# A waiting no-operation on the sync engine behind the last store of a scaled residual add

## The chip, the core and the metric

The kernel runs on one core of a Trainium2 chip. The metric is the device time of one execution in microseconds (us). A time is the median of several runs. Beside it stands one execution under the hardware profiler, which gives the views quoted here.

## The reference

```python
B, S, D = 512, 32, 640        # x, fx: (512, 32, 640) bfloat16; alpha: (1,) bfloat16

def reference(x, fx, alpha):
    return x + alpha * fx
```

One multiply and one add for each element. `x` and `fx` are read once and the output is written once: 20.97 MB each, 62.92 MB in all.

## The kernel before

The 512 x 32 rows are laid over the chip's 128 partitions, so that each partition holds 81920 consecutive elements of `x`, of `fx` and of the output. These are cut into five units of 16384 elements (`UNIT`), 32 KB a partition and 4 MB in all for each unit.

There are two pools of large tiles with two buffers each: `wide`, whose tiles hold two units of `x`, and `fs`, whose tiles hold one unit of `fx`. `x` comes in three loads, of units 0 and 1, of units 2 and 3, and of unit 4. `fx` comes in five loads, one for each unit. The vector engine computes `fx * alpha + x` in one instruction for each unit (line 59) and writes the result over the `x` tile. The result leaves in three stores, cut like the loads of `x`: `store(0, 2)`, `store(2, 2)` and `store(4, 1)` (line 71). The value of alpha is loaded alone (line 76), spread over the 128 partitions by a matmul with a row of ones (line 80), and copied for the vector engine (line 82).

All DMAs, loads and stores alike, are issued by the sync engine (SP) through one queue. The order of the instructions on each engine is written out by hand: the body stands under `tc.manual_schedule()`, and the loop over the units is unrolled in the source (lines 73 to 99). What the kernel doesn't write are the waits. The framework puts them in from the use of the tiles: an instruction waits on semaphores, which landed DMAs and finished instructions count up. A DMA adds 16 to its semaphore, one for each of the 16 DMA engines. An instruction that needs more waits than it can carry gets further waiting instructions ahead of it, which the trace shows as `EVENT_SEMAPHORE`.

Behind the body the framework adds a closing part of its own, for which no line of the kernel's body stands. Its records carry line 124, where the framework's context is opened and left. On the sync engine it waits for everything that the program has in flight or has counted, the last store among it; then come a barrier over all five engines, the clearing of the semaphores by GpSimd (POOL), and a second barrier. Records of the opening part carry line 113.

The lines that the change touches: `load_x` (49) and `load_f` (55) issue the loads, `compute` (59) the multiply-add, `store` (71) the stores; the unrolled order follows from line 73 on and ends with `store(4, 1)`.

Of the kernel before, what the change touches and what calls it, by code (L numbers as in the profile page):

```python
# [1 line left out]

# [4 lines left out]

ACT = mybir.ActivationFunctionType
ALU = mybir.AluOpType
F32 = mybir.dt.float32  # L10
BF16 = mybir.dt.bfloat16

UNIT = 16384
P = 128


@with_exitstack
def kernel(
    ctx: ExitStack,
    tc: tile.TileContext,  # L20
    x: bass.AP,
    fx: bass.AP,
    alpha: bass.AP,
    out: bass.AP,
):

    nc = tc.nc  # L30
    xv = x.flatten_outer_dims().rearrange("(p n) d -> p (n d)", p=P)
    fxv = fx.flatten_outer_dims().rearrange("(p n) d -> p (n d)", p=P)
    ov = out.flatten_outer_dims().rearrange("(p n) d -> p (n d)", p=P)
    assert xv.shape[1] == 5 * UNIT

    consts = ctx.enter_context(tc.tile_pool(name="consts", bufs=1))
    psum = ctx.enter_context(tc.tile_pool(name="psum", bufs=1, space=bass.MemoryType.PSUM))
    wide = ctx.enter_context(tc.tile_pool(name="wide", bufs=2))
    fs = ctx.enter_context(tc.tile_pool(name="fs", bufs=2))
    ctx.enter_context(tc.manual_schedule())  # L40

    xt, ft = {}, {}

    def cols(u, n):
        return slice(u * UNIT, (u + n) * UNIT)

    def load_x(u, n):
        t = wide.tile([P, 2 * UNIT], x.dtype, tag="x", name="x_t")
        nc.sync.dma_start(out=t[:, : n * UNIT], in_=xv[:, cols(u, n)])  # L49
        for i in range(n):  # L50
            xt[u + i] = (t, i)

    def load_f(u):
        ft[u] = fs.tile([P, UNIT], fx.dtype, tag="f", name="f_t")
        nc.sync.dma_start(out=ft[u][:], in_=fxv[:, cols(u, 1)])  # L55

    def compute(u):
        t, i = xt[u]
        nc.vector.scalar_tensor_tensor(  # L59
            out=t[:, i * UNIT : (i + 1) * UNIT],  # L60
            in0=ft[u][:],
            scalar=a_f[:],
            in1=t[:, i * UNIT : (i + 1) * UNIT],
            op0=ALU.mult,
            op1=ALU.add,
        )

    def store(u, n):
        t, i = xt[u]
        assert i == 0  # L70
        nc.sync.dma_start(out=ov[:, cols(u, n)], in_=t[:, : n * UNIT])

    load_x(0, 2)

    a_1 = consts.tile([1, 1], alpha.dtype, name="a_1")
    nc.sync.dma_start(out=a_1[:], in_=alpha[None, :])  # L76
    ones = consts.tile([1, P], alpha.dtype, name="ones")
    nc.vector.memset(ones[:], 1.0)  # L78
    a_ps = psum.tile([P, 1], F32, name="a_ps")
    nc.tensor.matmul(a_ps[:], ones[:], a_1[:], start=True, stop=True)  # L80
    a_f = consts.tile([P, 1], F32, name="a_f")
    nc.vector.tensor_copy(out=a_f[:], in_=a_ps[:])  # L82

    load_f(0)
    load_f(1)
    load_x(2, 2)
    compute(0)
    load_f(2)
    compute(1)
    store(0, 2)  # L90
    load_f(3)
    load_x(4, 1)
    compute(2)
    load_f(4)
    compute(3)
    store(2, 2)
    compute(4)
    store(4, 1)


# [1 line left out]
_INS = ['x', 'fx', 'alpha']  # L102
_OUTS = [((512, 32, 640), 'bfloat16')]


# [23 lines left out]
```

## Time and profile before

| | us |
|---|---|
| time, median of 3 runs (lowest to highest) | 152.76 (152.31 to 152.86) |
| the profiled execution's own time | 152.47 |
| its span, from the first to the last instruction of the program | 150.7 |
| vector engine busy in it | 86.7 |
| issue of the last store | 138.08 |
| its landing, when the last of 16 DMA engines has counted it | 149.63 |
| landing of the store before it, `store(2, 2)` | 139.95 |

The span leaves out 1.8 us of the execution's own time, which lie before the program's first instruction and after its last. In the views an engine's name with a small q (SPq) means its sequencer, which waits, issues DMAs and handles barriers and doesn't count as busy. A group's line gives the source line, the engine, the operation, the count, and durations; a view of one source line gives durations in ns as min/median/max and the first and last start in us, rounded to tenths. The profile's chain of waits is followed back from the last instruction that an engine itself executes, and so begins before the closing part. For a DMA, "to landing" is the time from its issue by the queue to its last count.

The order in which the sync queue issues its DMAs, with their start in us: `x` units 0 and 1 (0.73), alpha (1.17), `fx` 0 and 1 (1.55, 1.94), `x` units 2 and 3 (2.82), `fx` 2 (50.08), `store(0, 2)` (67.28), `fx` 3 (67.68), `x` unit 4 (91.48), `fx` 4 (91.92), `store(2, 2)` (118.48), `store(4, 1)` (138.08).

### The profile page before, as it was taken

Reading aid. Unit: us, or ns where it says so; the run is one execution under the profiler, and the core shown is the slowest. Engines: PE = TensorE matmul, PEld = TensorE weight load, DVE = VectorE, ACT = ScalarE, POOL = GpSimd, SP = SyncE. Lnnn points to the kernel's source line nnn. Section 1 sums busy time; section 2 is a strip of 40 time slices with the busy share of each in tenths; the row PEclk is TensorE's granted clock in tenths of the full one; section 3 lists DMA queues with packets and bytes.
Section 4 is the critical chain, followed back from the end, with each engine's and each line's share of the span. In section 5 each row is a group of like instructions: output and inputs, shape, how many; then the busy total and the mean of one; then the engine's idle time right before and its main releaser. Section 6 shows DMA issues by size and latency. Waiting matters only on the chain.

```text
span 150.7 us, 75 instructions
## 1 busy us (share of the span) xinstructions
PE 0.2 (0%) x1; PEld 0.1 (0%) x1; DVE 86.7 (58%) x7; POOL 0.2 (0%) x4
## 2 busy tenths in 40 slices
PE   0000000000000000000000000000000000000000
PEld 0000000000000000000000000000000000000000
DVE  0000000039999999980899970019999499996000
POOL 0000000000000000000000000000000000000000
DMA  8899899999999896999899989999999999989993
GB/s 278 383 452 470 365 418 417 426 426 444 478 452 487 348 557 278 426 452 478 348 522 417 417 365 418 435 418 426 444 435 470 487 435 400 470 365 391 435 426 139
DMA packets 1586, 62.92 MB, mean 418 GB/s; under 512 B 178, under 2 KB 178, under 8 KB 178
## 3 DMA queue, kind: packets, MB, share of 16 engines
q1 hardware_dynamic: 1586, 62.92, 97.5%
HBM read 41.94 MB, written 20.97 MB: 417 GB/s over the span
## 4 chain that ended last, share of the span: by engine, by line
DMA 56%; DVE 34%; SPq 1%; issue 0%; DVEq 0%
DMA f_t<-in_fx_dram 40%; DVE x_t L59 34%; DMA out_dram<-x_t 16%; SPq L49 0%; SPq L76 0%; DVEq L59 0%; SPq L55 0%
## 5 line engine op out<-in xcount | busy, mean ns | idle before, releaser
L59 DVE SCALAR_TENSOR_TENSOR x_t<-f_t,a_f,x_t 128x16384 bf16<-128x16384 bf16 x5 | 86.3, 17284 | 29.0 <-DMA f_t<-in_fx_dram 29.0
L82 DVE COPY a_f<-a_ps 128x1 f32<-128x1 f32 x1 | 0.2, 157 | 21.6 <-PE a_ps L80 21.6
L78 DVE MEMSET ones<- 1x128 bf16 x1 | 0.2, 165 | 0.8 <-PEq L113 0.8
L80 PE MATMUL a_ps<-a,ones 1*128 1x1 bf16 x1 | 0.2, 158 | 22.4 <-DMA a<-in_alpha_dram 22.4
L113 POOL MEMSET const-uint8-127<- 128x1 uint8 x1 | 0.1, 102 | 0.0
L113 POOL MEMSET const-bfloat16-1.0<- 128x1 bf16 x1 | 0.1, 101 | 0.0
L80 PEld LDWEIGHTS <-ones 1*128 1x128 bf16 x1 | 0.1, 98 | 1.0 <-DVE ones L78 1.0
L113 POOL MEMSET const-float32-0.0<- 128x1 f32 x1 | 0.1, 98 | 0.2 <-issue 0.2
L113 POOL MEMSET const-float32-1.0<- 128x1 f32 x1 | 0.1, 98 | 0.0
## 6 DMA issues: line engine op xcount, KB each, us to landing
f_t<-in_fx_dram SPq DMA_DIRECT2D x5, 4096.0 KB, 32.3
x_t<-in_x_dram SPq DMA_DIRECT2D x1, 4096.0 KB, 19.4
out_dram<-x_t SPq DMA_DIRECT2D x1, 4096.0 KB, 11.6
x_t<-in_x_dram SPq DMA_DIRECT2D x2, 40.5
out_dram<-x_t SPq DMA_DIRECT2D x2, 22.8
a<-in_alpha_dram SPq DMA_DIRECT2D x1, 0.0 KB
```

The lines of the kernel that those rows point to most:

```text
L59: nc.vector.scalar_tensor_tensor(out=t[:, i * UNIT : (i + 1) * UNIT], in0=ft[u][:], scalar=a_f[:], in1=t[:, i * UNIT : (i + 1) * UNIT], op ...
L78: nc.vector.memset(ones[:], 1.0)
L80: nc.tensor.matmul(a_ps[:], ones[:], a_1[:], start=True, stop=True)
L82: nc.vector.tensor_copy(out=a_f[:], in_=a_ps[:])
L113: nc = _bacc.Bacc("TRN2", target_bir_lowering=False, num_devices=1)
```

## The change

Every load, the matmul, the first two stores and the last multiply-add are kept in a list, `done`. Behind the last store the sync engine gets a no-operation that is made to depend on each of them: on all that the program does but the last store itself. (The copies and multiply-adds that aren't listed come earlier on the vector engine than the one that is.) `compute` and `store` now return the instruction that they make. Nothing that is loaded, computed or stored is changed.

```diff
+    done = []
...
     def load_x(u, n):
         t = wide.tile([P, 2 * UNIT], x.dtype, tag="x", name="x_t")
-        nc.sync.dma_start(out=t[:, : n * UNIT], in_=xv[:, cols(u, n)])
+        done.append(nc.sync.dma_start(out=t[:, : n * UNIT], in_=xv[:, cols(u, n)]))
...
     def load_f(u):
         ft[u] = fs.tile([P, UNIT], fx.dtype, tag="f", name="f_t")
-        nc.sync.dma_start(out=ft[u][:], in_=fxv[:, cols(u, 1)])
+        done.append(nc.sync.dma_start(out=ft[u][:], in_=fxv[:, cols(u, 1)]))
...
-    nc.sync.dma_start(out=a_1[:], in_=alpha[None, :])
+    done.append(nc.sync.dma_start(out=a_1[:], in_=alpha[None, :]))
...
-    nc.tensor.matmul(a_ps[:], ones[:], a_1[:], start=True, stop=True)
+    done.append(nc.tensor.matmul(a_ps[:], ones[:], a_1[:], start=True, stop=True))
...
-    store(0, 2)
+    done.append(store(0, 2))
...
-    store(2, 2)
-    compute(4)
+    done.append(store(2, 2))
+    done.append(compute(4))
     store(4, 1)
+
+
+    rest = nc.sync.nop(nofuse=True)
+    info = mybir.DependencyInfo(mybir.DependencyClass.Sync, mybir.DependencyReason.DATA)
+    for i in done:
+        tc.add_manual_dep(rest.ins, i.ins.name, info, reason="all but the last store")
```

More of the change, by code (lines that the diff above doesn't have):

```diff
@@ L54, in load_f @@
         ft[u] = fs.tile([P, UNIT], fx.dtype, tag="f", name="f_t")
-        nc.sync.dma_start(out=ft[u][:], in_=fxv[:, cols(u, 1)])
+        done.append(nc.sync.dma_start(out=ft[u][:], in_=fxv[:, cols(u, 1)]))
     def compute(u):
         t, i = xt[u]
-        nc.vector.scalar_tensor_tensor(
+        return nc.vector.scalar_tensor_tensor(
             out=t[:, i * UNIT : (i + 1) * UNIT],
@@ L70, in store @@
         assert i == 0
-        nc.sync.dma_start(out=ov[:, cols(u, n)], in_=t[:, : n * UNIT])
+        return nc.sync.dma_start(out=ov[:, cols(u, n)], in_=t[:, : n * UNIT])
     load_x(0, 2)
     a_1 = consts.tile([1, 1], alpha.dtype, name="a_1")
-    nc.sync.dma_start(out=a_1[:], in_=alpha[None, :])
+    done.append(nc.sync.dma_start(out=a_1[:], in_=alpha[None, :]))
     ones = consts.tile([1, P], alpha.dtype, name="ones")
```

## The prediction

> **What bounds the kernel now.** I read the page's DMA part first, then the costliest groups, then the waits of the sync engine's queue, then the end of the span in small windows. From the page:
>
> ```profile
> ## 3 DMA queue, kind: packets, MB, share of 16 engines
> q1 hardware_dynamic: 1586, 62.92, 97.5%
> ...
> L59 DVE SCALAR_TENSOR_TENSOR x_t<-f_t,a_f,x_t 128x16384 bf16<-128x16384 bf16 x5 | 86.3, 17284 | 29.0 <-DMA f_t<-in_fx_dram 29.0
> ```
>
> Transfers fill 97.5% of the 16 DMA engines' span; the vector engine works 86.3 us of 150.7 and waits 29.0 us for tiles of `fx`. So DMA sets the time, up to the last landing. The chain of waits on the page ends with the last vector instruction (138.06 us) and says nothing of what follows, so I asked for the last 12.6 us separately. First the record of the last store (the view of line 71, from 130 us on), then the closing stretch by windows (columns: stretch, length, each engine's busy time, clock, DMA share, GB/s):
>
> ```profile
> L71 SPq DMA_DIRECT2D out_dram<-x_t x1: 344/344/344, 138.1 to 138.1; - x1
> ...
> DMA to landing us min/median/max: 11.6/11.6/11.6
> ```
>
> ```profile
> 138.40:149.60 11.20, 0.00 (x0) 0.00 (x0) 0.00 (x0) 0.00 (x0) 1.00 0.87 375
> 149.60:150.70 1.10, 0.00 (x0) 0.00 (x0) 0.00 (x0) 0.00 (x0) 1.00 0.00 0
> ```
>
> The store is issued at 138.08 and lands at 149.63. For 11.2 us the sync engine has nothing to do. Then follows 1.1 us in which no engine works and no byte moves: only the program's closing on line 124. The waits of the sync engine's queue say what opens it:
>
> ```profile
> SPq L124 <- DMA out_dram<-x_t: 11.2, 1, 11.2
> SPq L124 <- PEq L124: 0.6, 2, 0.4
> ```
>
> and line 124 in two short windows (149.60 to 149.95, 149.95 to 149.99) what it consists of (duration in ns min/median/max, first and last start):
>
> ```profile
> L124 SPq EVENT_SEMAPHORE  x1: 17/17/17, 149.7 to 149.7; - x1
> L124 SPq EVENT_SEMAPHORE  x4: 28/28/28, 149.7 to 149.9; - x4
> L124 SPq DRAIN  x1: 7/7/7, 150.0 to 150.0; - x1
> ```
>
> One wait for the last store, four instructions with two waits each, and a drain that carries a tenth wait. The unrounded starts in the trace's records are 149.650, 149.709, 149.770, 149.835, 149.896 and 149.961; the next instruction, the drain that reports the queue to the closing barrier, starts at 150.020. All nine other semaphores had long been complete (the latest is the store of units 2 and 3, landed 139.95), yet each instruction takes its step of (149.961 - 149.650) / 5 = 0.062 us, because they stand in the queue behind the wait for the last store.
>
> **The change part by part.** *The list `done`, the added `return`s:* Python only. No instruction for the chip, so 0.
>
> *The no-operation on the sync engine.* It brings new waits, for at most nine semaphores, those of everything but the last store: the loads of `x`, `fx` and alpha, the matmul, both earlier stores, the last multiply-add. Its own record is in no row. The nearest are the drains and waits above: 7 to 28 ns long, a step of 0.062 us. At two waits an instruction nine of them take four waiting instructions and the no-operation itself, five steps or 0.31 us, at most six or 0.37. It is issued after the last store's issue (138.08 + 0.34 = 138.42), waits until 139.95 for the earlier store, and is done by 140.3 at the latest. The cover is the last store's flight, until 149.63; 9.3 us of it are left over. Behind it in the sync engine's queue stands only the closing on line 124, which waits for the landing anyway. No DMA, no tile and no other engine waits for it. On the path: 0. Without that cover it would cost its 0.31 to 0.37 us.
>
> *What it lets go of.* If the closing then waits for the last store alone, that wait fits on the drain, which can start at about 149.65 where the first wait now starts. Five steps go: 149.961 - 149.650 = 0.311 us. The barrier, the clearing of semaphores and the second barrier (150.020 to the end, 0.67 us) shift forward unchanged: the other four engines' drains are long reached. Bounds: nothing goes if the closing repeats its waits (0); if one wait more is left, say for the no-operation's own count, four steps go (0.25); more than the five steps cannot go, as the rest answers to other engines. Taken: 0.31.
>
> Sum, against the profiled execution: 152.47 us in all, 150.7 of it span; 152.47 - 0.31 = 152.16, span 150.4. That execution was 0.29 below the median of the runs (152.76, from 152.31 to 152.86). The middle of all four executions is (152.47 + 152.76) / 2 = 152.6, less 0.31 is 152.3; the median less 0.31 is 152.45. I go between: **152.4 us**.
>
> A rule that speaks against any gain is in the Trainium skill, Perfetto Trace Analysis, section Identifying Performance Opportunities: improving a kernel generally means improving its most-contended engine. By that rule alone, with DMA untouched, the forecast would be no gain, 152.6 to 152.76. The last window's row, DMA share 0.00 for 1.1 us, shows a place where that engine is not what is waited for, and there I follow the row.
>
> **The rivals.** *The closing repeats its waits.* What the program does with a wait already made must be read off the queues. For repetition: four of the closing's waits repeat, to the same value, what this very queue had waited for before. The records name the semaphores: 106 and 101 by the wait of line 55 at 91.86 us, 107 by the load at 91.49, 105 by the wait of line 71 at 92.34, 99 by the last store; the closing asks again for 105, 106 and 107 unchanged, and for 99 at the last store's value. So what DMA issues of this queue have seen is not credited to the closing drain. Against: within the body, waits are not repeated. The `fx` load at 67.68 needs the second multiply-add finished and carries no wait for it, since the store before it did; the vector engine waits once for the first `x` tile and uses it twice. The simplest reading is that DMA issues and the engine's own instructions keep separate accounts, and a no-operation belongs, with the drain, to the second. I hold that likelier, at two to one. If it is wrong, the no-operation is hidden and nothing goes: 152.6 to 152.76, say 152.7.
>
> *The no-operation gets ahead of the last store.* Slower: one wait in the wrong place. The store would then be issued only once the earlier store has landed, at 139.95 plus a step or two instead of 138.08. Its 11.55 us of flight shift whole, for with the engines free its first data packets started 0.84 us after the issue (138.92 in the packets' records). Landing at about 151.55, so +1.92, less 0.31 of the closing: 152.6 + 1.6 = 154.2. It decides from the point at which the no-operation starts before 138.08. For it: `done` holds nothing that keeps it behind the last store. Against: every DMA of the sync queue starts in the order in which the source has it, and the no-operation is written last.
>
> *More than the five steps.* Faster by over 0.5% (0.76 us) would need 0.45 us of the 0.67 us of barrier too. The page shows no mechanism; only the scatter of the runs (0.55 us from end to end) can make it look so.
>
> **How the numbers follow.** Closing shortened by four or five steps: 0.63. Closing repeats its waits: 0.29. No-operation ahead of the store: 0.03. More than the five steps, or something else: 0.05. A measurement of this kernel can tell about 0.5% (0.76 us) from no change; both likely cases lie within it (0.2% and 0). So: within 0.5%, 0.87. Faster by more, 0.09: most of it the first case with the scatter's help, as a run at the low end, 152.31 - 0.31 = 152.0, is just at the bound. Slower by more, 0.04: the order rival and a rest.
>
> The range: at the low end the lowest run less six steps, 152.31 - 0.37 = 151.9; at the high end the highest run with no saving, 152.86, rounded up to 152.9. It holds the first two cases with their scatter and leaves the other two out.
>
> **What would show it.** Right: on line 124 of the sync queue the two-wait instructions are gone after 149.6 us and stand between 138.4 and 140.3 instead, on the no-operation's line; from the last landing to the span's end about 0.75 us instead of 1.06; the last store still issued at 138.1 with 11.6 us to landing; everything before that as it was. The second case: the same four instructions with two waits still start after the last landing, beside a no-operation near 140. The order rival: the last store issued near 140.0. The forecast is wrong if the step of 0.062 us is not what a satisfied wait costs but comes from the landing itself, or if a no-operation's waits disturb the transfers in flight: then the last store's 11.6 us would change.

## The result and the profile after

| | before | after |
|---|---|---|
| time, median of 18 runs (us) | 152.47 (152.11 to 152.87) | 152.17 (151.82 to 152.48) |
| ratio, 95% interval | | 0.9977 [0.9969, 0.9985] |
| span of the profiled execution (us) | 150.69 | 150.47 |
| issue of the last store, its landing (us) | 138.08, 149.63 | 138.11, 149.72 |
| closing: last landing to the end of the span (us) | 1.060 | 0.749 |

By the ratio the kernel became 0.35 us faster (0.23 to 0.47 by its interval), by the difference of the two medians 0.30. That is 0.2%: within the 0.5% named as the bound of no change, though the interval leaves no change out. The closing is 0.311 us shorter. The spans differ by 0.22 us only, because this execution's last landing came 0.09 us later.

What bounds the kernel is as it was. From the page of the changed kernel (its lines are numbered higher; the multiply-add is now line 60, the stores line 72, the no-operation line 102, the closing line 131; in the experiments the closing's number moves again):

```profile
q1 hardware_dynamic: 1586, 62.92, 97.7%
...
L60 DVE SCALAR_TENSOR_TENSOR x_t<-f_t,a_f,x_t 128x16384 bf16<-128x16384 bf16 x5 | 86.3, 17284 | 29.0 <-DMA f_t<-in_fx_dram 29.0
```

Same bytes, same busy time, same 29.0 us of waiting for `fx`. The last store, from the view of its line:

```profile
L72 SPq DMA_DIRECT2D out_dram<-x_t x1: 344/344/344, 138.1 to 138.1; - x1
...
DMA to landing us min/median/max: 11.6/11.6/11.6
```

It starts 0.03 us later and flies 0.06 us longer; two executions of the changed kernel itself (the first experiment) differ by 0.42 and 0.08. The windows behind it (columns as in the prediction):

```profile
138.45:149.72 11.27, 0.00 (x0) 0.00 (x0) 0.00 (x0) 0.00 (x0) 1.00 0.87 372
149.72:150.50 0.78, 0.00 (x0) 0.00 (x0) 0.00 (x0) 0.00 (x0) 1.00 0.00 0
```

The stretch without any transfer was 1.1 us long and is now 0.78. Where the waiting went, by the sync queue's waits:

```profile
SPq L131 <- DMA out_dram<-x_t: 9.5, 1, 9.5
SPq L102 <- DMA out_dram<-x_t: 1.5, 1, 1.5
SPq L131 <- PEq L131: 0.6, 2, 0.4
```

Before, line 124 waited 11.2 us in one piece. Now the no-operation's line waits 1.5 us for the earlier store and the closing 9.5 us for the last one. (A `DRAIN` is one more instruction of the engine's queue; in the closing's records one carries a wait, and the next counts up the barrier's semaphore.) The views of lines 102 and 131 (the second from 149.60 to 149.79) show the instructions (ns min/median/max, first and last start):

```profile
L102 SPq EVENT_SEMAPHORE  x5: 28/28/1493, 138.5 to 140.2; - x5
```

```profile
L131 SPq DRAIN  x1: 7/7/7, 149.7 to 149.7; - x1
```

Five waiting instructions with two waits each stand under the store's flight, and the one of 1493 ns holds the real wait. Behind the landing (149.722) one drain is left, at 149.739; the drain that reports to the barrier follows at 149.797, 0.058 us later. Before, from the first wait to that drain were six steps, 0.370 us. The rest of the closing takes 0.674 us in both. The no-operation has no record of its own: both traces hold 75 instructions, and what differs is the place of five waiting instructions and the carrier of the wait for the last store, which has gone from the first waiting instruction to the drain.

### The profile page after: what moved, and what is told of

The parts are those of the page before. It is cut to its first block, busy times and chain, and to the rows that moved or that the text cites. A ratio compares the mean times of both kernels' runs of the same rounds, so it can differ in the third digit from the quotient of the medians.

```text
span 150.5 us, 75 instructions
## 1 busy us (share of the span) xinstructions
PE 0.2 (0%) x1; PEld 0.1 (0%) x1; DVE 86.7 (58%) x7; POOL 0.2 (0%) x4
## 4 chain that ended last, share of the span: by engine, by line
DMA 56%; DVE 34%; SPq 1%; issue 0%; DVEq 0%
DMA f_t<-in_fx_dram 40%; DVE x_t L60 34%; DMA out_dram<-x_t 16%; SPq L50 0%; SPq L77 0%; DVEq L60 0%; SPq L56 0%
```

## The experiments

The first theory was that of the prediction: a satisfied wait costs the step of its instruction, and the no-operation moves five such steps under the last store. Each experiment edits the changed kernel, unless it says otherwise. "Closing" is always the time from the last landing to the end of the span, from the trace. Each ratio is to the kernel before as it ran beside that experiment (medians of 152.31 to 152.36 us). The intervals of the ratios are about as wide as the whole gain, 0.2%: they tell a full gain from none, but not three steps from five. That is read from the closings.

| run | closing (us) | time (us) | ratio to before, 95% |
|---|---|---|---|
| the changed kernel again | 0.748 | 152.16 | 0.9978 [0.9965, 0.9991] |
| waits for the last store too | 1.048 | 152.32 | 1.0002 [0.9991, 1.0012] |
| on GpSimd's queue | 1.059 | 152.50 | 1.0008 [0.9997, 1.0020] |
| a drain in its place | 0.750 | 152.00 | 0.9981 [0.9969, 0.9993] |
| ahead of the last store | 0.746 | 153.66 | 1.0090 [1.0074, 1.0106] |
| waits for one half | 0.749 | 152.09 | 0.9987 [0.9976, 0.9997] |
| eight loads more, no no-operation | 1.141 | 152.31 | 0.9999 [0.9990, 1.0008] |
| eight loads more, with it | 0.820 | 152.07 | 0.9983 [0.9971, 0.9996] |
| four loads more, no no-operation | 0.813 | 152.03 | 0.9981 [0.9967, 0.9994] |
| waits for the other half | 0.814 | 152.00 | 0.9977 [0.9964, 0.9990] |

**The changed kernel again.** Expected:

> The changed kernel itself, again, beside the other three. Theory (five waiting steps leave the end of the path): closing, from the last landing to the end of the span, 0.75 us as in the first profile against 1.06 before; time 0.31 us under before, ratio 0.998. Rival (the measured 0.3 us is scatter or comes from another place, say from the transfers): ratio anywhere within 0.999 to 1.001, or a gain with a last landing that is earlier by as much.

The closing came out the same to 1 ns and the ratio too, while the last landing was at 149.22 in this execution and 149.72 in the first. So the landing's time scatters by half a microsecond from one execution to the next, more than the effect, and the closing does not.

**Waiting for the last store too.**

```diff
-    store(4, 1)
+    done.append(store(4, 1))
```

> The no-operation waits for the last store too. Theory: its waits now stand behind the last landing, so nothing is hidden: a closing of 1.06 us again (five waiting instructions and two drains, in other places), time as before, ratio 0.999 to 1.001. Rival (the gain comes from the waits standing ahead of the closing part, wherever their time lies, for instance because the closing's own instructions are fetched or started later or earlier): closing near 0.75 us and ratio 0.998 again.

The sync queue's waits in this run:

```profile
SPq L102 <- DMA out_dram<-x_t: 11.1, 1, 11.1
SPq L133 <- PEq L133: 0.6, 2, 0.4
```

and the instructions of the no-operation's line:

```profile
L102 SPq EVENT_SEMAPHORE  x5: 27/28/11117, 138.2 to 149.6; - x5
```

All waits stand ahead of the closing part, which asks for nothing more, and yet the gain is gone: the first pair (its records name the last store's semaphore) holds the queue to the landing, and four pairs and two drains follow it. It is not the place in the program that counts but what lies under the flight. The theory's figure, 1.06, was 1.048.

**On GpSimd's queue, and a drain instead.**

```diff
-    rest = nc.sync.nop(nofuse=True)
+    rest = nc.gpsimd.nop(nofuse=True)
```

> The same no-operation with the same dependences, on GpSimd's queue instead of the sync engine's. Theory (what counts is which queue has waited): the closing on the sync engine repeats all its waits, 1.06 us, ratio 0.999 to 1.001; GpSimd has its five waits hidden near 140 us. Rival (that any engine has waited is enough): closing 0.75 us, ratio 0.998.

```profile
SPq L133 <- DMA out_dram<-x_t: 11.2, 1, 11.2
```

```profile
L133 SPq EVENT_SEMAPHORE  x5: 17/28/28, 149.4 to 149.7; - x5
```

Both read as before the change (the second is the closing's line from 138 to 149.79), and so does the closing. The framework credits the sync engine's closing with nothing that GpSimd has waited for. Then the other way round, the same queue with another carrier:

```diff
-    rest = nc.sync.nop(nofuse=True)
+    rest = nc.sync.drain(fusable=False)
```

> A drain of the sync engine in place of the no-operation, with the same dependences. Theory: any instruction of this queue that takes the waits will do: closing 0.75 us, ratio 0.998, a drain near 140.3 us in the records. Rival (the no-operation is special): closing 1.06 us.

```profile
L102 SPq DRAIN  x1: 7/7/7, 140.2 to 140.2; - x1
```

As the theory had it: closing 0.750, and the drain stands at 140.25 us.

**Ahead of the last store.** The three lines of the no-operation stand before `store(4, 1)`.

> The no-operation stands ahead of the last store instead of behind it. This is the order rival of the prediction, made on purpose. Theory: the store is issued after the earlier store's landing, near 140.1 to 140.3 instead of 138.1, and lands 11.6 us or a little less later; closing 0.75 us; time 152.5 + 1.9 to 2.2 - 0.3 = 154.1 to 154.4, ratio 1.011 to 1.013. Rival (the last store's packets queue behind the earlier store's anyway, so a later issue is hidden in part): landing later by under 1.2 us, time under 153.4.

The last store in this run, from the view of its line:

```profile
L72 SPq DMA_DIRECT2D out_dram<-x_t x1: 343/343/343, 139.9 to 139.9; - x1
...
DMA to landing us min/median/max: 11.1/11.1/11.1
```

Slower by 1.35 us (153.66 against 152.31), between the two expectations. The earlier store landed at 139.68 in this execution, the remaining waits took their steps, and the issue followed at 139.93, 0.25 us after that landing; but the flight shrank from 11.55 to 11.12. Windows of the kernel before, then of this one, show where the time went (a window counts a packet where it starts):

```profile
138.10:139.00 0.90, 0.00 (x0) 0.00 (x0) 0.00 (x0) 0.00 (x0) 1.00 0.69 291
139.00:140.00 1.00, 0.00 (x0) 0.00 (x0) 0.00 (x0) 0.00 (x0) 1.00 0.61 262
```

```profile
138.10:139.00 0.90, 0.00 (x0) 0.00 (x0) 0.00 (x0) 0.00 (x0) 1.00 0.01 0
139.00:140.00 1.00, 0.00 (x0) 0.00 (x0) 0.00 (x0) 0.00 (x0) 1.00 0.00 0
```

By the packets' records, the 16 DMA engines finish the earlier store between 138.71 and 139.60 in the kernel before, and those that finish after 138.92, when the first packets of the last store are ready, go on to it within 0.01 us. With the late issue they finish between 138.50 and 139.30 and stand idle until 140.77 to 140.92. That is the loss. The flight is shorter because its start no longer waits for an engine that is still busy: the last of them began 1.52 us after the issue before (139.60 against 138.08), and 0.99 us after it here (140.92 against 139.93). Without the scatter of the earlier landing: issue 139.95 + 0.25 - 138.08 = 2.12 us later, flight 0.43 shorter, closing 0.31 shorter, together 1.38.

**One half of the waits.** The no-operation depends on five things alone.

```diff
-    for i in done:
+    for i in done[2:3] + done[9:]:
```

> The no-operation waits for the matmul, the load of x unit 4, the load of fx unit 4, the second store and the last multiply-add alone; four landings more are left to the closing. Theory, by count: the closing keeps two instructions with two waits each and the drain, three steps in place of six, so 3 x 0.062 = 0.19 us go: closing 0.87 us, ratio 0.9988. Rival (a gain of all or nothing, for a closing that repeats or doesn't repeat its waits as a whole): closing 0.75 or 1.06 us.

This missed. The view of the closing's line (from 138.00 to 149.64):

```profile
L133 SPq EVENT_SEMAPHORE  x2: 28/28/28, 140.0 to 140.1; - x2
L133 SPq DRAIN  x1: 7/7/7, 149.6 to 149.6; - x1
```

Three instructions are left in the closing, as counted. But the two pairs stand ahead of the wait for the last store, which is now on the drain, so they pass near 140 us under its flight. All five steps went, not three: closing 0.749 where the count had 0.87. The ratio of this run, 0.9987, is the one that the count had forecast, but its interval (0.9976 to 0.9997) holds both. The count of waits was the wrong measure.

**Eight semaphores more.** The kernel before with eight small loads, and the same loads with the no-operation.

```diff
+    for k in range(8):
+        t = consts.tile([1, 1], alpha.dtype, name=f"more_{k}")
+        done.append(nc.gpsimd.dma_start(out=t[:], in_=alpha[None, :]))
     load_f(0)
```

> The kernel before with eight loads of alpha more, 2 bytes each, issued early by GpSimd into tiles of their own that nothing reads. They bring eight semaphores more to the closing. Theory: nine waiting instructions and the drain instead of five and the drain, four steps more, 4 x 0.062 = 0.25 us: closing 1.31 us, time 0.25 us over before (ratio 1.0016) or more by what the eight loads cost elsewhere. Rival (a satisfied wait is free and the 0.06 us belong to the landing): closing 1.06 us.

> The same eight loads, and the no-operation of the change, which waits for them too. Theory: nine steps are hidden under the last store, the closing is one drain: 0.75 us, 9 x 0.062 = 0.56 us under the kernel with the eight loads and no no-operation, 0.31 us under before if the loads cost nothing elsewhere. Rival (what is hidden is a fixed amount of 0.3 us): closing 1.0 us.

Without the no-operation the closing has ten instructions ahead of the barrier, and should have cost four steps more. Its line from 138.0 to 149.3, then from 149.3 to 149.78:

```profile
L130 SPq EVENT_SEMAPHORE  x4: 17/28/28, 138.3 to 139.8; - x4
...
L130 SPq EVENT_SEMAPHORE  x5: 28/28/28, 149.4 to 149.7; - x5
L130 SPq DRAIN  x1: 7/7/7, 149.7 to 149.7; - x1
```

The framework has put the last store's wait in the middle: four pass early, and from the last store's wait on stand six, as before the change. Of the closing's 1.141 us, 0.081 more than before, the sync queue has no part: its stretch up to the barrier's drain is 0.365 against 0.370. The rest is the barrier and the clearing, 0.759 against 0.674. With the no-operation all nine pairs pass early:

```profile
L105 SPq EVENT_SEMAPHORE  x9: 28/28/28, 138.5 to 140.3; - x9
```

The closing was 0.820, and so 0.32 us shorter than with the loads alone, not 0.56. From the landing to the barrier's drain it takes 0.075 us, as in the changed kernel; the 0.07 us above that kernel's closing are again barrier and clearing. A second miss, of the same cause, and the rival's "fixed amount" named the size but not the reason.

**A new theory, tried without any no-operation.** What costs is the number of instructions that stand behind the wait for the last store. If so, the order alone is enough. In the records of these closings the drain keeps one wait, the others form a list, the vector engine's semaphore first and then the DMAs' by number, and they are paired from the two ends of the list, the innermost first; the last store's semaphore stands in the first wait before the change because it falls in the list's middle. Four loads more on the sync queue turn the semaphores on:

```diff
+    for k in range(4):
+        t = consts.tile([1, 1], alpha.dtype, name=f"more_{k}")
+        nc.sync.dma_start(out=t[:], in_=alpha[None, :])
     compute(0)
```

> No no-operation: the kernel before with four loads of alpha more, 2 bytes each, on the sync engine's queue behind its first five loads, into tiles that nothing reads. The semaphores of the queue's DMAs are given out by turns, and four DMAs more make the last store's semaphore the one that the closing asks for in its last two-wait instruction instead of its first wait. New theory (what costs is the number of instructions that stand behind the wait for the last store, not the number of waits in the closing): the same ten waits in the same six instructions, but four of them pass near 138 to 140 us, so 4 x 0.062 = 0.25 us go: closing 0.81 us, time 0.25 us under before if the four loads cost nothing elsewhere. The first theory's count (each wait left in the closing costs its step): closing 1.06 us, ratio 1.000 or above.

Its closing's line from 137 to 149.42, then from 149.42 to 149.55:

```profile
L130 SPq EVENT_SEMAPHORE  x4: 17/28/28, 138.3 to 139.8; - x4
...
L130 SPq EVENT_SEMAPHORE  x1: 28/28/28, 149.5 to 149.5; - x1
L130 SPq DRAIN  x1: 7/7/7, 149.5 to 149.5; - x1
```

Ten waits in six instructions, as before the change, yet four have passed when the store lands: closing 0.813, and the time falls to 0.9981 [0.9967, 0.9994] of before. And the other half of the list, where count and place differ again:

```diff
-    for i in done:
+    for i in done[5:9]:
```

> The no-operation waits for the other four only: the load of x units 2 and 3, the loads of fx units 2 and 3, the first store. Six waits stay in the closing, in four instructions, the one with the last store's wait third, ahead of the drain. New theory (place, not number): two of the four pass early, the drain is the one step behind the wait, so four of five steps go as in e9: closing 0.81 us, ratio about 0.9984. By count: four instructions left of six, two steps go: closing 0.94 us, ratio 0.9992.

Its closing's line from 138 to 140, then from 149 to 149.45:

```profile
L133 SPq EVENT_SEMAPHORE  x2: 17/22/28, 138.3 to 139.7; - x2
...
L133 SPq EVENT_SEMAPHORE  x1: 28/28/28, 149.4 to 149.4; - x1
L133 SPq DRAIN  x1: 7/7/7, 149.4 to 149.4; - x1
```

Closing 0.814 where the count had 0.94. With one instruction behind the wait in the changed kernel (its barrier drain), two in these two runs and six before, the closings are 0.749, 0.813 and 1.060: 0.064 us for the first step more, 0.247 / 4 = 0.062 for each of the others.

No run went below the changed kernel's closing by more than 3 ns. Behind the landing it has one wait left and the barrier; whether either can be shortened was not tried.

## Why the prediction was right

*The sum.* Five steps of 0.062 us were to go, 0.311 us; the closing fell from 1.060 to 0.749, which is 0.311. The runs say 0.35 (0.23 to 0.47). That the time fell inside the range, 151.9 to 152.9, proves little: the range held the case of no gain as well. It is the closing and the place of the waits in the trace that tell the two apart.

*The level.* 152.4 was forecast and 152.17 measured. The gain had its size; the base did not. Three runs had a median of 152.76 and eighteen have 152.47. The middle of the four executions then at hand, 152.6, was nearer; going between it and the median of three runs moved the forecast away from the result.

*The no-operation costs nothing.* Right: the wait holds to 140.1, the last of its five instructions starts at 140.22, and 9.5 us of cover were left. "Nine of them" was one short: the no-operation also asks for the earlier count of the last store's semaphore, so it carries ten waits in five instructions. Its own record was to be a sixth step at most; there is none.

*The two accounts.* The likelier reading held. The no-operation waits anew for the semaphores 105, 106, 107 and 99, which DMA issues of its own queue had waited for, and the closing then drops them. That another engine's waits earn no credit is shown by the run on GpSimd. How the framework keeps its accounts inside is read off the queues, not seen.

*The rival that the closing repeats its waits* would have left 1.06 us and fell with the first profile.

*The order rival* had the right mechanism and too high a price: +1.6 us forecast, +1.35 measured. The term at fault is "its 11.55 us of flight shift whole": the flight took 11.12, since before it had waited for engines still at work on the earlier store. The issue, "at 139.95 plus a step or two", was off the other way by less: 0.25 us behind that landing.

*What the working did not see.* It counted the waits that "stand in the queue behind the wait for the last store" and was right, since that wait stood first and the change left it alone; that its place could move was not considered. In the changed kernel both readings take five steps away, so its result can't tell them apart. The half list and the eight loads, expected by count, did: the steps behind the landing follow the place of that one wait. So the bound "if one wait more is left", four steps, holds only for a wait that stands behind it; in the half list four waits more were left, and all five steps went.

## What to carry to other kernels

Look at what stands behind the last landing: instructions whose waits are long satisfied still cost a step each (0.062 us here) when they are queued behind the one that waits. Move them under the flight of the last transfer, on the same queue; an instruction that only waits is enough, and so is an order in which the late wait comes last. Whatever is put there must not get ahead of that transfer's issue, which cost 1.35 us here, four times the gain. All this was seen on one kernel; no other was tried.

## What had not been expected of the hardware

With eight more semaphores in use GpSimd's range clear took 136 ns instead of 93, its drain ahead of that 93 to 107 ns instead of 70, and the closing from the barrier's drain on 0.745 to 0.759 us instead of 0.674. In both runs GpSimd had also issued the eight loads, so whether the number of semaphores does it or that issuing is not shown. Four more loads on the sync queue, which took no new semaphore, left it at 93 and 0.673. A satisfied two-wait instruction takes longer on GpSimd's queue than on the sync engine's: 43 ns and a step of 0.087 us in the run on GpSimd, against 28 ns and 0.062 us.
